# Stores of converted weight pieces queued two steps later, their raw weights fetched four products earlier, and the conversions of w_out spaced out

## The chip, the cores and the metric

The kernel runs as one program on one core of a Trainium2 chip. The metric is the device time of an execution in microseconds (us), as the median of three runs. TensorE (PE) multiplies; VectorE (DVE) and ScalarE (ACT) prepare operands and empty PSUM; SyncE (SP) issues every DMA.

## What is computed

A small attention in both directions between tokens and state, then two feed-forward layers over the 4352 rows that it gives. The change lies in the second of these layers and in the hand-over to it.

```python
def reference(x, state, w_in1, w_out1, s, b, w_in2, w_out2):
    x = attention(x, state)                     # 8*(512+32) = 4352 rows of 512
    h = np.maximum(x @ w_in1, 0.0)              # 512 -> 2048
    x = (s * (h * h) + b) @ w_out1              # 2048 -> 512
    h = np.maximum(x @ w_in2, 0.0)
    return (h * h) @ w_out2                     # what the changed code prepares and reads
```

## The kernel before, in words

Everything is fp32 to the caller. Each factor of a matmul is split into a rounded part "hi" and a remainder "lo" (hi is a copy on ACT, lo a subtraction on DVE), and three matmuls, hi by hi, hi by lo and lo by hi, stand for one.

The second layer works on 34 tiles of 128 rows in six parts of six tiles (the last has four). For each part the first matrix, w_in2, is gone through in eight **units** u of 256 columns (`units`, part by part; unit i of the whole list is written (i, m) with the step m inside it). A unit multiplies by Strassen's scheme in Winograd's form: seven **products** of half-size blocks, in the order `PRODUCTS`, one product being one step, m = 0 to 6. A product is six matmuls of 384 columns (L634). The products share two PSUM banks (psa and psb in turn), and some products add onto the bank of an earlier one, so product m = 3 can start only when DVE has taken product m = 1 out of its bank (the sum `r`, in the group DVE r L713), and m = 6 only when m = 4 has been taken out (`v`, DVE v L713). The first product of a unit goes into the bank of product m = 5 of the unit before, and the second (m = 1) into the bank of m = 6 of the unit before, which DVE empties with an add into `t`.

Between products PE does matmuls that are already prepared, its "flow": at the second of every two steps it takes ten or eleven matmuls with w_out2 (`mm2_second`, L679), which multiply what the unit before gave. So PE runs two products, some flow, two products, some flow. At the hand-over (unit 0) the flow is the last 24 matmuls of the first layer (L478), four of which are left for the first step of unit 1.

The weights of a unit are seven **pieces** (128x256, hi and lo beside each other), sums and differences of four blocks of w_in2. In the first part they have to be made. For units 0 and 1 that happens at steps of the first layer's last batch (`s8 + n`), for units u = 2 to 7 while unit u-1 is worked on:

- `sums_load(u)` (L527): two DMAs of 256 KB bring the raw blocks `ws` from HBM into tiles of a pool with four buffers. It was queued at (u-2, 6).
- `sums_add(u, n)` (L542, tiles `wt` and `ws`): three sums on DVE at (u-1, 0), one more at (u-1, 3).
- `sums_hi(u, m)` (L550, ACT) at (u-1, m), `sums_lo(u, m)` (L554, DVE) at (u-1, m+1). With the lo part, in the same function, went the DMA that stores the piece to HBM (L555, `w2s`), since parts 2 to 6 read the pieces from there (`w_load`, L563 and L566).

The pieces of even units lie in one set of places (behind the x operands in `xw`), those of odd units in another (`xw odd`).

The second matrix, w_out2, has been brought to fp32 in HBM earlier. It comes back in eight pieces of 512 KB, `load_w2` (L208, tile `o2f`), and is split by `cut`: `o2h` on ACT and `o2l` on DVE (L110, L111; 128x1024). Piece p holds the weights that unit p's results meet, and PE first reads it in unit p+1.

Nothing is reordered by a scheduler: every engine does its instructions in the order in which the code is run, and each of the engines' queues, SP's of DMAs too, waits at its head. The tables of steps (`at_step(step, fn, rank)` for the first layer, `then(i, m, fn)` and `between` for the second) thus set the order on DVE, ACT and SP at once.

Of the kernel before, what the change touches and what calls it, by code (L numbers as in the profile page):

```python
# [42 lines left out]
NF = DFF // P  # L43
NQ = 4
# [9 lines left out]
PRODUCTS = (1, 6, 2, 5, 7, 3, 4)  # L54
# [7 lines left out]
def attn_mlp2(ctx: ExitStack, tc: tile.TileContext, xT, xn, st, w_in1, w_out1, w_in2, w_out2, s_in, b_in, out):  # L62
# [43 lines left out]
    def raw4(name):  # L106
        return rawp.tile([P, 2, 512], F32, tag="raw", name=name)

    def split(hi, lo, src):
        nc.scalar.activation(out=hi, in_=src, func=ACTF.Copy)  # L110
        nc.vector.tensor_tensor(out=lo, in0=src, in1=hi.bitcast(F32), op=ALU.subtract)  # L111
# [53 lines left out]
    def w_tiles(key, q):  # L165
        if (key, q) not in W:
            W[key, q] = (w8([P, 4, 512], f"{key}h{q}"), w8([P, 4, 512], f"{key}l{q}"))
        return W[key, q]
# [37 lines left out]
    def load_w2(key, q, p):  # L206
        raw = raw4(f"{key}f{q}{p}")
        nc.sync.dma_start(out=raw, in_=w2_dr[key, q][:, 2 * p : 2 * p + 2, :])  # L208

        def cut():  # L210
            hi, lo = w_tiles(key, q)
            split(hi[:, 2 * p : 2 * p + 2, :], lo[:, 2 * p : 2 * p + 2, :], raw)

        return cut
# [301 lines left out]
    def w_at(e, m):  # L516

        return xw[m][:, 4 * TH :] if e == 0 else xw["odd", m // 4][:, m % 4 * 512 : m % 4 * 512 + 512]
# [3 lines left out]
    def sums_load(u):  # L522

        c0 = u % 2 * 2 * P
        sums[u] = [op.tile([P, 2, 2, P], F32, tag="o", name=f"ws{u}") for _ in range(2)]
        for d, t in enumerate(sums[u]):
            nc.sync.dma_start(  # L527
                out=t.rearrange("p i f c -> p i (f c)"),
                in_=w2_dr["i2", u // 2][:, 2 * d : 2 * d + 2, c0 : c0 + 2 * P],
            )  # L530

    def sums_add(u, n):

        (a11, a21), (a12, a22) = [[t[:, :, f, :] for f in range(2)] for t in sums[u][:2]]
        if n == 0:
            sums[u].append(an1.tile([P, 2, 2, P], F32, tag="an", name=f"wt{u}"))
        s1, s2 = (sums[u][2][:, i] for i in range(2))
        out, x, y, fn = (
            (s1, a21, a22, ALU.add), (s2, s1, a11, ALU.subtract),
            (a21, a11, a21, ALU.subtract), (a12, a12, s2, ALU.subtract),  # L540
        )[n]
        nc.vector.tensor_tensor(out=out, in0=x, in1=y, op=fn)  # L542
        sums[u, "src"] = {1: a11, 2: a12, 3: a12, 4: a22, 5: s1, 6: s2, 7: a21}

    def sums_view(u, m):
        return w_at(u % 2, m).rearrange("p (h i c) -> p h i c", h=2, i=2), sums[u, "src"][PRODUCTS[m]]

    def sums_hi(u, m):
        w, v = sums_view(u, m)
        nc.scalar.activation(out=w[:, 0], in_=v, func=ACTF.Copy)  # L550

    def sums_lo(u, m):
        w, v = sums_view(u, m)
        nc.vector.tensor_tensor(out=w[:, 1], in0=v, in1=w[:, 0].bitcast(F32), op=ALU.subtract)  # L554
        nc.sync.dma_start(out=w2s_dr[u][:, m, :], in_=w_at(u % 2, m).bitcast(F32))  # L555

    def w_load(i, m):
# [13 lines left out]
    def x_view(n, m):  # L571
        th = half(n)
        return xw[m][:, : 4 * th].rearrange("p (h i t) -> p h i t", h=2, i=2)
# [35 lines left out]
    def x_hi(n, m, i):  # L609
        nc.scalar.activation(out=x_view(n, m)[:, 0, i], in_=X["t", i][PRODUCTS[m]], func=ACTF.Copy)  # L610

    def x_lo(n, m, i):
        v = x_view(n, m)
        nc.vector.tensor_tensor(
            out=v[:, 1, i], in0=X["t", i][PRODUCTS[m]], in1=v[:, 0, i].bitcast(F32), op=ALU.subtract
        )
# [205 lines left out]
    def at_step(i, fn, rank=5):  # L822

        side.setdefault(i, []).append((rank, len(side.get(i, ())), fn))
# [5 lines left out]
    def step(j, f):  # L830
        return place[j, 0] + f
# [19 lines left out]
    rank = {att_sr: 0, att_tp: 0, att_sc: 0, att_put: 2, att_an: 3, att_turn: 3, att_exp: 5, att_norm: 5}  # L851
    for b in range(1, B):
# [6 lines left out]
        for q in range(NQ):  # L859

            n = base + 4 * q + 5 if b > 1 else (1, 12, 16, 20)[q]
# [28 lines left out]
    s8 = step(B, 0)  # L890
# [23 lines left out]
    for m in range(len(PRODUCTS)):  # L914
        n = s8 + (2, 2, 3, 5, 6, 9, 10)[m]
        for i in range(2):
            at_step(n, lambda m=m, i=i: x_hi(0, m, i), 8)
            at_step(n + 1, lambda m=m, i=i: x_lo(0, m, i), 6)
    for u, at0, steps in ((0, 4, (5, 5, 6, 6, 7, 9, 9)), (1, 11, (12, 12, 13, 13, 14, 14, 15))):
        at_step(s8 + 3, lambda u=u: sums_load(u), 9.5)  # L920
        for n in range(3):
            at_step(s8 + at0, lambda u=u, n=n: sums_add(u, n), 8)
        for m, n in enumerate(steps):
            at_step(s8 + n, lambda u=u, m=m: sums_hi(u, m), 9.5)
            at_step(s8 + n + 1, lambda u=u, m=m: sums_lo(u, m), 6)

        at_step(s8 + steps[2] + 1, lambda u=u: sums_add(u, 3), 7)
    between = {}
    w_pieces = {}
    for q in range(NQ):  # L930
        for h in range(2):

            load = lambda q=q, h=h: w_pieces.update({(q, h): load_w2("o2", q, h)})
            cut = lambda q=q, h=h: w_pieces.pop((q, h))()
            if q < 1:
                at_step(s8 + 11 + h, load, 9)
                at_step(s8 + 13 + h, cut, 9)
            else:
                between.setdefault((q - 1, 3 * h), []).append(load)
                between.setdefault((q - 1, 3 * h + 3), []).append(cut)  # L940

    def then(i, m, fn):
        between.setdefault((i + m // len(PRODUCTS), m % len(PRODUCTS)), []).append(fn)

    for u in range(2, NF // 2):
        then(u - 2, 6, lambda u=u: sums_load(u))
        for n in range(3):
            then(u - 1, 0, lambda u=u, n=n: sums_add(u, n))
        for m in range(len(PRODUCTS)):
            then(u - 1, m, lambda u=u, m=m: sums_hi(u, m))  # L950
            then(u - 1, m + 1, lambda u=u, m=m: sums_lo(u, m))
            if m == 2:
                then(u - 1, 3, lambda u=u: sums_add(u, 3))

# [10 lines left out]
    for f in range(1, NF):  # L965
        i = v_at[f] + (f >= VA)
# [128 lines left out]
```

## Time and profile before

| | us |
|---|---|
| median of three runs | 1420.15 (1417.08 to 1421.92) |
| the profiled execution | 1422.37 |
| its span in the trace | 1420.6 |

The profile is that of one execution. Times in it are counted from the start of the span. PE is the array's matmuls, PEld its weight loads, SPq the queue of DMAs on SP. "idle before <- X" names what ended an engine's wait. The granted clock (PEclk) is 1.00 when TensorE runs at 2.4 GHz and 0.50 at 1.2 GHz.

### The profile page before, as it was taken

Reading aid. Unit: us, or ns where it says so; the run is one execution under the profiler, and the core shown is the slowest. Engines: PE = TensorE matmul, PEld = TensorE weight load, DVE = VectorE, ACT = ScalarE, POOL = GpSimd, SP = SyncE. Lnnn points to the kernel's source line nnn. Section 1 sums busy time; section 2 is a strip of 40 time slices with the busy share of each in tenths; the row PEclk is TensorE's granted clock in tenths of the full one; section 3 lists DMA queues with packets and bytes.
Section 4 is the critical chain, followed back from the end, with each engine's and each line's share of the span. In section 5 each row is a group of like instructions: output and inputs, shape, how many; then the busy total and the mean of one; then the engine's idle time right before and its main releaser. Section 6 shows DMA issues by size and latency. Waiting matters only on the chain.

```text
span 1420.6 us, 20203 instructions
## 1 busy us (share of the span) xinstructions
PE 1380.5 (97%) x7770; PEld 1164.7 (82%) x7770; DVE 764.6 (54%) x1495; ACT 759.3 (53%) x1492; POOL 0.7 (0%) x7
## 2 busy tenths in 40 slices
PE   4999999999999999999988999999999999999998
PEld 2777777777777777889877889999999999989897
DVE  7888645555556766446655554353435344443533
ACT  4777656566666656557644543354345335433543
POOL 0000000000000000000000000000000000000000
PEclk7899999999999999999999999999999999999999
DMA  7365232423324142204563555445435544543652
GB/s 248 102 221 182 89 122 61 137 90 102 125 75 143 54 155 72 90 0 142 171 206 113 194 165 169 118 117 166 142 111 171 172 118 118 163 141 105 214 152 72
DMA packets 88863, 188.48 MB, mean 133 GB/s; under 512 B 8640, under 2 KB 26048, under 8 KB 86208
## 3 DMA queue, kind: packets, MB, share of 16 engines
q1 hardware_dynamic: 88768, 187.21, 41.6%
q8 instruction: 61, 1.00, 0.3%
q14 instruction: 34, 0.28, 0.1%
HBM read 144.18 MB, written 42.99 MB: 132 GB/s over the span
## 4 chain that ended last, share of the span: by engine, by line
PE 92%; DVE 3%; DMA 2%; ACT 1%; issue 1%; SPq 0%; DVEq 0%
PE acc L478 26%; PE o L679 25%; PE m L634 22%; PE h L448 14%; PE S L260 2%; DMA ws<-i 2%; PE sr L413 1%; PE sc L260 1%; PE S L288 1%; PE tp L393 0%; DMA o2f<-o 0%; DMA xT<-xT 0%; ACT sc L647 0%; SPq L527 0%; ACT o2h L110 0%
## 5 line engine op out<-in xcount | busy, mean ns | idle before, releaser
L478 PE MATMUL acc<-g,o1h 128*128 128x512 f32 (+1 forms) x1152 | 341.5, 379 | 0.0
L478 PEld LDWEIGHTS acc<-g,o1h 128*128 128x128 f32 x1152 | 211.7, 188 | 41.8 <-issue 2.2
L478 PE MATMUL acc<-g,o1l 128*128 128x512 f32 (+1 forms) x576 | 217.7, 378 | 0.4 <-DVE o1l L189 0.4
L448 PE MATMUL h<-aT,S 128*128 128x512 f32 x768 | 202.6, 399 | 5.8 <-DVE aT L387 3.2
L634 PE MATMUL m<-xw 128*128 128x384 f32 (+1 forms) x1008 | 185.9, 331 | 9.5 <-DVE r L713 8.0
L448 PEld LDWEIGHTS h<-aT,S 128*128 128x128 f32 x768 | 142.0, 189 | 61.0 <-issue 12.3
L634 PEld LDWEIGHTS m<-xw 128*128 128x128 f32 x1008 | 172.9, 190 | 18.1 <-DVE r L713 9.0
L647 ACT ACTIVATE sc<-sc 128x384 f32<-128x384 f32 (+1 forms) x144 | 72.7, 505 | 156.7 <-DVE sc L713 155.2
L461 DVE TENSOR_TENSOR g<-r,g 128x512 fp32r<-128x512 f32 (+1 forms) x144 | 94.8, 659 | 109.9 <-ACT g L457 109.9
L455 ACT ACTIVATE r<-h 128x512 f32<-128x512 f32 (+1 forms) x144 | 82.2, 571 | 124.5 <-PE h L448 124.4
L647 ACT ACTIVATE v<-m 128x384 f32<-128x384 f32 (+1 forms) x96 | 45.4, 473 | 152.1 <-PE m L634 151.6
L478 PEld LDWEIGHTS acc<-g,o1l 128*128 128x128 f32 x576 | 108.5, 188 | 21.3 <-DVE o1l L189 0.9
L679 PE MATMUL o<-o2h,xw('g', 0)_6303 128*128 128x512 f32 x364 | 122.3, 396 | 0.0
L679 PE MATMUL o<-o2h,xw('g', 1)_6304 128*128 128x512 f32 x364 | 121.2, 393 | 0.0
L679 PE MATMUL o<-o2h,xw('g', 2)_6305 128*128 128x512 f32 x360 | 120.1, 394 | 0.0
L713 DVE TENSOR_TENSOR v<-m,r 128x384 f32<-128x384 f32 (+1 forms) x48 | 25.7, 535 | 158.5 <-PE m L634 158.5
L634 PE MATMUL m<-xw,xw('odd', 0)_6178 128*128 128x384 f32 (+1 forms) x576 | 107.6, 328 | 3.1 <-DVE r L713 3.1
L634 PEld LDWEIGHTS m<-xw,xw('odd', 0)_6178 128*128 128x128 f32 x576 | 98.2, 188 | 8.0 <-DVE r L713 4.4
L457 ACT ACTIVATE g<-r 128x512 fp32r<-128x512 f32 (+1 forms) x144 | 87.7, 609 | 4.6
L456 ACT ACTIVATE r<-r 128x512 f32<-128x512 f32 (+1 forms) x144 | 87.7, 609 | 4.6
L111 DVE TENSOR_TENSOR S<-S,S 128x512 fp32r<-128x512 f32 x54 | 34.8, 687 | 91.4 <-ACT S L110 91.4
L634 PE MATMUL m<-xw,xw('odd', 1)_6179 128*128 128x384 f32 (+1 forms) x432 | 79.5, 327 | 0.6 <-DVE v L713 0.6
(146 smaller groups left out, 1900.0 us busy)
## 6 DMA issues: line engine op xcount, KB each, us to landing
xw<-w2s SPq DMA_DIRECT2D x140, 256.0 KB, 2.8
xw('odd', 0)_6178<-w2s SPq DMA_DIRECT2D x20, 1024.0 KB, 4.9
xw('odd', 1)_6179<-w2s SPq DMA_DIRECT2D x20, 768.0 KB, 4.3
i1r<-w_in SPq DMA_DIRECT2D x16, 512.0 KB, 4.7
xn<-xn SPq DMA_DIRECT2D x8, 1024.0 KB, 8.8
o1r<-w_out SPq DMA_DIRECT2D x16, 512.0 KB, 4.6
x<-ot SPq DMA_DIRECT2D x32, 256.0 KB, 3.1
i2r<-w_in SPq DMA_DIRECT2D x16, 512.0 KB, 5.3
```

What stands on the lines that cost most here:

```text
L111: nc.vector.tensor_tensor(out=lo, in0=src, in1=hi.bitcast(F32), op=ALU.subtract)
L260: nc.tensor.matmul(out=outs[r][k * NS : (k + 1) * NS], lhsT=state[rows, r, k, :], rhs=moving(rows, k), start=True, stop=True, skip_group_c ...
L448: nc.tensor.matmul(out=hp, lhsT=l_, rhs=r_, start=(i == 0), stop=(i == len(ops) - 1))
L455: nc.scalar.activation(out=r, in_=hp, func=ACTF.Relu)
L456: nc.scalar.activation(out=r, in_=r, func=ACTF.Square)
L457: nc.scalar.activation(out=g[:, 0], in_=r, func=ACTF.Copy)
L461: nc.vector.tensor_tensor(out=g[:, 1], in0=r, in1=g[:, 0].bitcast(F32), op=ALU.subtract)
L478: nc.tensor.matmul(out=o, lhsT=l_, rhs=r_, start=(opens and i == 0), stop=(closes and i == 2))
L634: nc.tensor.matmul(out=o, lhsT=w[:, a, k, :], rhs=x[:, b, k, :], start=(start and k + a + b == 0), stop=(k + a == 2), skip_group_check=True,)
L647: nc.scalar.activation(out=c, in_=src, func=func)
L679: nc.tensor.matmul(out=acc2[t], lhsT=l_, rhs=r_, start=(fa == 0 and e == 0), stop=(fa == NF - 1 and e == 2))
L713: add = lambda o, x, y: nc.vector.tensor_tensor(out=o, in0=x, in1=y, op=ALU.add)
```

## The change

The store of a piece becomes a function of its own, `sums_store`, which is put two steps behind the lo part. `sums_load(u)` moves from (u-2, 6) to (u-2, 2). The eight pieces of w_out2 are loaded and split at steps from a written table of (load, split) pairs, in which a number below zero is a step of the first layer and u = 7 stands for the steps of a unit; before, a loop put them at every third step. No instruction is added or removed and no size changes.

```diff
@@ -552,6 +552,8 @@
         w, v = sums_view(u, m)
         nc.vector.tensor_tensor(out=w[:, 1], in0=v, in1=w[:, 0].bitcast(F32), op=ALU.subtract)
+
+    def sums_store(u, m):
         nc.sync.dma_start(out=w2s_dr[u][:, m, :], in_=w_at(u % 2, m).bitcast(F32))
@@ -916,39 +918,46 @@
+    def behind(n, fn, rank):
+
+        if n < NF:
+            at_step(s8 + n, fn, rank)
+        else:
+            then(0, n - NF, fn)
+
     for u, at0, steps in ((0, 4, (5, 5, 6, 6, 7, 9, 9)), (1, 11, (12, 12, 13, 13, 14, 14, 15))):
         at_step(s8 + 3, lambda u=u: sums_load(u), 9.5)
         for m, n in enumerate(steps):
             at_step(s8 + n, lambda u=u, m=m: sums_hi(u, m), 9.5)
-            at_step(s8 + n + 1, lambda u=u, m=m: sums_lo(u, m), 6)
+            behind(n + 1, lambda u=u, m=m: sums_lo(u, m), 6)
+            behind(n + 3, lambda u=u, m=m: sums_store(u, m), 9.9)
-    for q in range(NQ):
-        for h in range(2):
-
-            load = lambda q=q, h=h: w_pieces.update({(q, h): load_w2("o2", q, h)})
-            cut = lambda q=q, h=h: w_pieces.pop((q, h))()
-            if q < 1:
-                at_step(s8 + 11 + h, load, 9)
-                at_step(s8 + 13 + h, cut, 9)
-            else:
-                between.setdefault((q - 1, 3 * h), []).append(load)
-                between.setdefault((q - 1, 3 * h + 3), []).append(cut)
+    u = len(PRODUCTS)
+    for p, (n, k) in enumerate((
+        (11 - NF, 14 - NF), (12 - NF, 1), (0, 5), (3, u + 1), (6, u + 4), (u + 2, 2 * u), (u + 5, 2 * u + 3),
+        (2 * u + 1, 2 * u + 6),
+    )):
+        q, h = p // 2, p % 2
+        behind(n + NF, lambda q=q, h=h: w_pieces.update({(q, h): load_w2("o2", q, h)}), 9)
+        behind(k + NF, lambda q=q, h=h: w_pieces.pop((q, h))(), 9)
     for u in range(2, NF // 2):
-        then(u - 2, 6, lambda u=u: sums_load(u))
+        then(u - 2, 2, lambda u=u: sums_load(u))
         for n in range(3):
             then(u - 1, 0, lambda u=u, n=n: sums_add(u, n))
         for m in range(len(PRODUCTS)):
             then(u - 1, m, lambda u=u, m=m: sums_hi(u, m))
             then(u - 1, m + 1, lambda u=u, m=m: sums_lo(u, m))
+            then(u - 1, m + 3, lambda u=u, m=m: sums_store(u, m))
```

What this does to SP's queue shows in unit 1. A row is a DMA, destination first; `w2s_2` are the stored pieces of unit 2 and `ws3` the raw blocks of unit 3. Before:

```order
L555 DMA w2s_2_119<-xw0_5737 128x512
L555 DMA w2s_2_119<-xw1_5738 128x512
L208 DMA o2f21_6507<-o2_2_115 128x1024
L555 DMA w2s_2_119<-xw2_5739 128x512
L555 DMA w2s_2_119<-xw3_5871 128x512
L555 DMA w2s_2_119<-xw4_5872 128x512
L555 DMA w2s_2_119<-xw5_6031 128x512
L527 DMA ws3_6578<-i2_1_110 128x2x256
L527 DMA ws3_6579<-i2_1_110 128x2x256
```

And in the changed kernel:

```order
L504 DMA x1_8_133<-ot_6430 128x256
L504 DMA x1_8_133<-ot_6436 128x256
L208 DMA o2f21_6488<-o2_2_115 128x1024
L527 DMA ws3_6492<-i2_1_110 128x2x256
L527 DMA ws3_6493<-i2_1_110 128x2x256
L557 DMA w2s_2_119<-xw0_5737 128x512
L557 DMA w2s_2_119<-xw1_5738 128x512
L208 DMA o2f30_6551<-o2_3_116 128x1024
```

The load of `ws3` stood behind six stores of unit 2's pieces and now stands ahead of all of them.

On DVE the second place is the start of unit 2, where product m = 1 is taken out (`r`, L713 before and L715 after), with the three sums for unit 3 ahead of it. Before:

```order
L661 TENSOR_TENSOR xw('g', 2)_6305<-sc,xw('g', 2)_6305 128x384
L644 SCALAR_TENSOR_TENSOR t_6544<-t_6544 128x384
L111 TENSOR_TENSOR o2l_6504<-o2f_6507,o2h_6503 128x1024
L554 TENSOR_TENSOR xw_6031<-ws_6413,xw_6031 128x256
L554 TENSOR_TENSOR xw_6032<-ws_6413,xw_6032 128x256
L542 TENSOR_TENSOR wt_6599<-ws_6578,ws_6579 128x256
L542 TENSOR_TENSOR wt_6599<-wt_6599,ws_6578 128x256
L542 TENSOR_TENSOR ws_6578<-ws_6578 128x2x128
L713 TENSOR_TENSOR r<-m_6604,v 128x384
```

And in the changed kernel:

```order
L663 TENSOR_TENSOR xw('g', 2)_6297<-sc,xw('g', 2)_6297 128x384
L646 SCALAR_TENSOR_TENSOR t_6546<-t_6546 128x384
L554 TENSOR_TENSOR xw_6026<-ws_6341,xw_6026 128x256
L111 TENSOR_TENSOR o2l_6532<-o2f_6488,o2h_6531 128x1024
L554 TENSOR_TENSOR xw_6027<-ws_6341,xw_6027 128x256
L542 TENSOR_TENSOR wt_6597<-ws_6492,ws_6493 128x256
L542 TENSOR_TENSOR wt_6597<-wt_6597,ws_6492 128x256
L542 TENSOR_TENSOR ws_6492<-ws_6492 128x2x128
L715 TENSOR_TENSOR r<-m_6602,v 128x384
```

The `o2l` moved behind one lo part. It now belongs to step (2, 0) instead of (1, 6), and so does its `o2h`, which stood on ACT among the hi parts of (1, 6) and stands there now behind the copy of unit 2's first product:

```order
L649 ACTIVATE v<-m_6580 128x384
L649 ACTIVATE t_6562<-t_6562 128x384 x2
L649 ACTIVATE xw('g', 0)_6295<-t_6562 128x384
L649 ACTIVATE xw('g', 0)_6295<-t_6546 128x384
L110 ACTIVATE o2h_6531<-o2f_6488 128x1024
L550 ACTIVATE xw('odd', 0)_6176<-ws_6492 128x256
```

Five instructions of ACT, which begin with that copy (`v`), now come between the first product of the unit and `o2l`. The third place is the end of unit 0 on DVE, where `t` empties the bank that unit 1's second product takes. Before:

```order
L713 TENSOR_TENSOR sc<-m_6340,r 128x384
L713 TENSOR_TENSOR t_6382<-v 128x384
L503 TENSOR_SCALAR ot<-acc_5762,s_sb 128x256
L713 TENSOR_TENSOR t_6406<-m_6364,r 128x384
L661 TENSOR_TENSOR xw('g', 0)_6303<-sc,xw('g', 0)_6303 128x384
L644 SCALAR_TENSOR_TENSOR t_6382<-t_6382 128x384
L111 TENSOR_TENSOR o2l_6359<-o2f_6362,o2h_6358 128x1024
```

And in the changed kernel:

```order
L715 TENSOR_TENSOR sc<-m_6344,r 128x384
L715 TENSOR_TENSOR t_6382<-v 128x384
L503 TENSOR_SCALAR ot<-acc_5762,s_sb 128x256
L111 TENSOR_TENSOR o2l_6401<-o2f_6310,o2h_6400 128x1024
L715 TENSOR_TENSOR t_6410<-m_6364,r 128x384
L663 TENSOR_TENSOR xw('g', 0)_6295<-sc,xw('g', 0)_6295 128x384
L646 SCALAR_TENSOR_TENSOR t_6382<-t_6382 128x384
```

An `o2l` stood behind the add that empties product m = 6 into `t`; one stands ahead of it now.

## Rows read from the trace of the kernel before

**Rows 1.** The page: busy time of PE, share of the span, instructions.

```profile
PE 1380.5 (97%) x7770; PEld 1164.7 (82%) x7770; DVE 764.6 (54%) x1495; ACT 759.3 (53%) x1492; POOL 0.7 (0%) x7
```

**Rows 2.** Busy time by stretch: each engine, PEclk, DMA share, GB/s.

```profile
800.00:820.00 20.00, 20.00 (x99) 17.81 (x99) 11.95 (x26) 11.78 (x26) 0.00 (x0) 1.00 0.52 175
```

**Rows 3.** Waits of 640 to 820: total us, times, longest.

```profile
PE m L634 <- DVE r L713: 11.1, 6, 3.8
PE m L634 <- DVE v L713: 2.1, 2, 1.5
DVE wt L542 <- DMA ws<-i: 26.3, 6, 6.5
```

**Rows 4.** PE in order of time: start, us; in brackets the idle time before.

```profile
691.37 1.33 PE L634 MATMUL m<-xw 128*128 128x384 f32 x6 [1.46 <-DVE v L713]
...
719.76 2.29 PE L634 MATMUL m<-xw 128*128 128x384 f32 x6 [2.93 <-DVE r L713]
...
758.27 1.97 PE L634 MATMUL m<-xw 128*128 128x384 f32 x5 [3.77 <-DVE r L713]
...
794.25 1.31 PE L634 MATMUL m<-xw 128*128 128x384 f32 x6 [1.30 <-DVE r L713]
```

**Rows 5.** The same view: the first products of units 0, 4 and 8.

```profile
681.13 2.25 PE L634 MATMUL m<-xw 128*128 128x384 f32 x12
748.87 2.27 PE L634 MATMUL m<-xw 128*128 128x384 f32 x12
820.23 2.27 PE L634 MATMUL m<-xw 128*128 128x384 f32 x12
```

**Rows 6.** The chain that ended last, in order of time: start, us.

```profile
671.21 1.44 PE acc L478 x12
...
815.75 2.10 PE m L634 x12
817.86 2.31 PE o L679 x10
```

**Rows 7.** SP's queue in order of time, in unit 4.

```profile
740.98 9.02 SPq L555 DMA_DIRECT2D w2s<-xw  x6
750.05 0.99 SPq L527 DMA_DIRECT2D ws<-i  x2
```

**Rows 8.** DVE in order of time, in unit 4.

```profile
756.53 0.42 DVE L542 TENSOR_TENSOR wt<-ws,ws 128x256 f32<-128x256 f32 x1 [6.55 <-DMA ws<-i]
...
757.67 0.55 DVE L713 TENSOR_TENSOR r<-m,v 128x384 f32<-128x384 f32 x1
```

**Rows 9.** ACT and DVE in order of time, in unit 0.

```profile
688.53 1.06 ACT L110 ACTIVATE o2h<-o2f 128x1024 fp32r<-128x1024 f32 x1 [0.86 <-DMA o2f<-o]
...
689.62 1.23 DVE L111 TENSOR_TENSOR o2l<-o2f,o2h 128x1024 fp32r<-128x1024 f32 x1 [5.58 <-ACT o2h L110]
```

**Rows 10.** Busy time by stretch, behind two of the gaps.

```profile
719.76:724.00 4.24, 4.24 (x14) 3.83 (x15) 1.55 (x4) 2.16 (x5) 0.00 (x0) 0.62 0.56 180
758.27:764.00 5.73, 5.73 (x15) 4.96 (x16) 3.25 (x8) 2.32 (x6) 0.00 (x0) 0.51 0.36 137
```

**Rows 11.** ACT and DVE in order of time, at starts of units and splits.

```profile
751.62 0.94 ACT L647 ACTIVATE xw('g', 1)_6304<-t 128x384 fp32r<-128x384 f32 x2
...
723.45 1.04 ACT L110 ACTIVATE o2h<-o2f 128x1024 fp32r<-128x1024 f32 x1
...
724.52 1.23 DVE L111 TENSOR_TENSOR o2l<-o2f,o2h 128x1024 fp32r<-128x1024 f32 x1 [3.21 <-ACT o2h L110]
725.67 0.42 DVE L554 TENSOR_TENSOR xw('odd', 0)_6178<-ws,xw('odd', 0)_6178 128x256 fp32r<-128x256 f32 x1
```

**Rows 12.** PE and DVE in order of time, at the end of unit 0.

```profile
686.84 2.25 PE L634 MATMUL m<-xw 128*128 128x384 f32 x12
...
691.70 0.55 DVE L713 TENSOR_TENSOR sc<-m,r 128x384 f32<-128x384 f32 x1
...
695.26 1.23 DVE L111 TENSOR_TENSOR o2l<-o2f,o2h 128x1024 fp32r<-128x1024 f32 x1 [0.28 <-ACT o2h L110]
```

More of the change, by code (lines that the diff above doesn't have):

```diff
@@ L918, in attn_mlp2, with then @@
             at_step(n + 1, lambda m=m, i=i: x_lo(0, m, i), 6)
+    between = {}
+    def then(i, m, fn):
+        between.setdefault((i + m // len(PRODUCTS), m % len(PRODUCTS)), []).append(fn)
+    def behind(n, fn, rank):
[3 more added lines that the diff above has]
+            then(0, n - NF, fn)
     for u, at0, steps in ((0, 4, (5, 5, 6, 6, 7, 9, 9)), (1, 11, (12, 12, 13, 13, 14, 14, 15))):
@@ L924, in attn_mlp2 @@
             at_step(s8 + n, lambda u=u, m=m: sums_hi(u, m), 9.5)
-            at_step(s8 + n + 1, lambda u=u, m=m: sums_lo(u, m), 6)
+            behind(n + 1, lambda u=u, m=m: sums_lo(u, m), 6)
+            behind(n + 3, lambda u=u, m=m: sums_store(u, m), 9.9)
         at_step(s8 + steps[2] + 1, lambda u=u: sums_add(u, 3), 7)
-    between = {}
     w_pieces = {}
-    for q in range(NQ):
-        for h in range(2):
-            load = lambda q=q, h=h: w_pieces.update({(q, h): load_w2("o2", q, h)})
-            cut = lambda q=q, h=h: w_pieces.pop((q, h))()
-            if q < 1:
-                at_step(s8 + 11 + h, load, 9)
-                at_step(s8 + 13 + h, cut, 9)
-            else:
-                between.setdefault((q - 1, 3 * h), []).append(load)
-                between.setdefault((q - 1, 3 * h + 3), []).append(cut)
-    def then(i, m, fn):
-        between.setdefault((i + m // len(PRODUCTS), m % len(PRODUCTS)), []).append(fn)
+    u = len(PRODUCTS)
[6 more added lines that the diff above has]
+        behind(k + NF, lambda q=q, h=h: w_pieces.pop((q, h))(), 9)
     for u in range(2, NF // 2):
-        then(u - 2, 6, lambda u=u: sums_load(u))
+        then(u - 2, 2, lambda u=u: sums_load(u))
         for n in range(3):
```

## The prediction

> **What bounds the kernel now.** I read the page first: PE is busy 97% of the span [rows 1], so only time in which PE stands or runs at its lower clock can be won. The table of busy time by stretches of 20 us then shows where that is. From 800 us on PE is busy all the time at the granted clock 1.00 [rows 2], and so it is in the stretches ahead of 680; the losses that this change can reach lie in units 0 to 7. The waits of that stretch say what they are: PE waits for DVE's `r` six times, 11.1 us in all, and for DVE's `v` twice, 2.1 us, together 13.2; the one row that stands beside them is DVE's own wait for the raw blocks `ws`, six times, 26.3 us [rows 3]. There is one such wait for each of the units u = 2 to 7.
>
> PE in order of time gives the sizes of the gaps, from 1.30 to 3.77 us in the four shown [rows 4], and DVE in order of time the cause: `wt` began 6.55 us late, for the DMA of `ws`, and `r`, which PE waits for, stands right behind the three sums [rows 8]. SP's queue shows why the DMA was late: six stores held its head for 9.02 us, each until DVE had made its lo part, and the loads behind them were issued at 750.05, 6.5 us before `wt` could start [rows 7, 8]. One gap has another cause: at 691.37 PE waits for `v` [rows 4], which stood on DVE behind an `o2l` that waited 5.58 us for its `o2h`, and that for the DMA of `o2f` [rows 9].
>
> **What all of this costs.** I take it from starts, since the idle times in the trace count from modelled ends of matmuls. Without a wait twelve matmuls of a product take 2.10 us, ten of the flow 2.31, and twelve of the first layer's last batch 1.44 [rows 6]: 0.175, 0.231 and 0.12 us each. Unit 0 is 42 product matmuls and 20 of the first layer, 7.35 + 2.40 = 9.75 us. A later unit is 42 and 36 of the flow, 7.35 + 8.32 = 15.67; unit 1 has four of the first layer more, 16.15. Units 0 to 7 should take 9.75 + 16.15 + 6 x 15.67 = 119.9 us. They took 820.23 - 681.13 = 139.1 [rows 5]. So **19.2 us** are to be had. The parts fit: 13.2 us of gaps, then 4.24 x 0.38 + 5.73 x 0.49 = 1.6 + 2.8 = 4.4 us that the lower clock cost behind the two long gaps [rows 10], and some 0.2 us at each of the eight restarts.
>
> **The loads, part one.** `sums_load` goes four products earlier, 4 x 15.67 / 7 = 9.0 us, and the stores that held the queue now ask for lo parts that DVE made two steps (4.5 us) before. The longest that DVE waited was 6.55 us [rows 8], so a lead of 9.0 covers each of the six, with 2.4 us to spare, if SP is not held by something else. What stands ahead of `ws` now are stores of lo parts already made and one load of `o2f`; for unit 3 also the four stores of the first layer's last rows, made in step (1, 0), and for unit 5 the eight DMAs that bring the next part's x. I cost these at nothing: `ws3` is not used before (2, 0) and the rows are out seven steps earlier. If this cover fails, the old gap at that unit stays. The wait for a free buffer is no new one: unit u takes the buffers of u-2, done with at (u-2, 0), two steps ahead of its load. The stores themselves are 42 + 14 DMAs of 256 KB as before, and PE waits for none of them. So the six gaps go, with the clock that fell behind two of them, and the smaller wait for `v` in unit 1, in which DVE was still catching up.
>
> **The splits of w_out2, part two.** Piece 1 is split later, at (0, 1) instead of a step of the first layer, and piece 2 at (0, 5) instead of (0, 3), with a longer lead behind its load. That removes the 5.58 us wait and the gap at 691.37. The splits at (0, 1), (1, 1), (1, 4), (2, 3) and (2, 6) I cost at nothing: there `o2l` stands behind the `r` or `v` of its step, and PE has a flow of 2.3 us and a product of 1.05 before it asks for the next one. Without that cover each would cost the 1.15 us from the start of `o2l` to that of DVE's next instruction [rows 11]. Two do not hide.
>
> At **(2, 0)** the `o2h` stands behind five ACT instructions that start with the end of unit 2's first product, and `o2l`, the last lo part, the three sums and `r` follow. Unit 4 of the old trace has the same ACT instructions at the same place: two products start at 748.87, and the last two copies before ACT is free at 751.62 take 0.94 [rows 5, 11]. Counted from the start of the first product, o2h starts at 2.75 + 0.85 = 3.6 (the next instruction starts about 0.1 before the end in the trace); o2l 1.07 behind it, 4.67; the next DVE instruction 1.15 on, 5.82 [rows 11]; the lo part 0.34 (0.42 less that overlap), 6.16; from `wt` to `r` 1.14, 7.30; and product m = 3 starts 0.60 behind `r`, at 7.90 [rows 4, 8]. PE could start it after 2.10 + 2.31 + 1.05 = 5.46. So a new gap of **2.4 us** comes to unit 2. Its bounds are nothing, should ACT run ahead, and 2.4 + 2.8 = 5.2, should the clock fall as it did behind the gap at 758.27.
>
> At **(0, 5)** an `o2l` now stands ahead of `t`, which must empty the bank before unit 1's second product. In the old trace o2l began 3.56 us after `sc`, behind the same ACT work [rows 12]. In the new one `sc` follows product m = 5, which ends at 686.84 + 2.25 = 689.09, say 689.17. Then o2l at 692.73, `t` at 693.88 and the product, by the same 0.60, at 694.48. PE could have started it at 686.84 + 2.10, plus seven matmuls of the first layer (0.84), two products (2.10), four more of the first layer (0.48) and five of the flow (1.16): 693.52. A new gap of **1.0 us**, bounded by nothing and by the 1.46 that an `o2l` cost at this place before [rows 4].
>
> **The sum.** 19.2 - 2.4 - 1.0 = 15.8 us less. The profiled execution took 1422.37, 2.2 us above the median; it would come to 1406.6, and the median to 1420.15 - 15.8 = **1404.4**. Three runs of before lie 4.8 us apart, and 0.3% (4.3 us) is about what a measurement of this kernel can tell from no change.
>
> **The rivals.**
> *The new gaps do not come* (ACT is ahead at both places): 1420.15 - 19.2 = 1401.0. For it speaks that ACT is busy only 53% of the time [rows 1]; against it that both chains start with PE itself. Chance 0.20.
> *The clock falls behind the gap at (2, 0).* Behind 2.93 and 3.77 us the granted clock was 0.62 and 0.51 over the next 4 to 6 us [rows 4, 10], the lower level of 1.2 GHz for most of them; behind 1.30 and 1.46 it stayed. A gap of 2.4 lies between. Cost 1.6 to 2.8: 1406.0 to 1407.2. Chance 0.22. The Trainium skill, in "TensorE: Matmul & The Clock Gate", section "Part 1: The HAM clock gate", says that the lower clock is the default and that only activity lifts it, so that a matmul stream starts slowly again after idle time; by that rule the new gap would cost this more. The two long gaps agree with it, and the short ones show that it does not follow every pause.
> *The loads are still late at some units*: `ws3` behind the four row stores, `ws5` behind the eight loads of x. If both old long gaps stay, 2.93 + 3.77 with 4.4 of clock, 11.1 us of the gain are missing: 1415.5. Against it stand the seven and six steps (some 13 us) between those DMAs and the use. Chance 0.08; that nearly all six waits stay and the change does no more than remove the 691.37 gap, 1418 to 1420, has 0.03.
> *Slower.* A store that is two steps later reads its piece two steps longer. `sums_hi(u+2, m)` writes the same place, 14 steps behind hi(u, m), and must wait for it: 11 steps, 24.6 us, lie between the two now, 13 before. If SP came to lag by more than that, ACT would wait in each of the units, and to lose the 15.8 us and 4.3 more over six units it must lag by 24.6 + 3.4 = 28 us. The longest that SP stood for stores was 9.02 us [rows 7], while they still waited for fresh lo parts. Chance 0.02: 1425.
>
> **How the numbers follow.** The forecast has 0.45; with the rivals above that is 1.00. The range takes in the first two rivals at both ends, with 2 us below and some 4 above for a set of three runs and for part of one late load: 1399 to 1411. That leaves out late loads, the slower case and a little of the spread. Faster by over 0.3%: 0.94; within: 0.04; slower: 0.02.
>
> **What would show it.** In the new trace the row of DVE waiting for `ws` is gone or below 2 us in all; SP's loads of `ws` are issued in the middle of the unit ahead; PE has two gaps between 681 and 805, one of about 1.0 us at the second product of unit 1 behind `t`, one of about 2.4 at the fourth of unit 2 behind `r`, each with an `o2l` just before on DVE; the granted clock is 1.00 in units 3 to 7; and unit 8 starts at 820.23 - 15.8 = 804.4. Wrong would be: gaps at the fourth product of units 3 to 6 behind `wt`, or ACT waiting for a `w2s` store ahead of L550.

## The result and the profile after

The changed kernel takes **1405.8 us** (median of four runs, 1405.25 to 1406.81) against 1420.27 of the kernel before on the same chip: a ratio of 0.9902, with a 95% interval of 0.9883 to 0.992. The forecast was 1404.4. The profiled execution took 1405.25 us with a span of 1403.5.

The waits of the same stretch as in [rows 3], in the changed kernel (total us, times, longest). There is no row of DVE waiting for `ws` any more, and PE's waits, 13.2 us before, are two:

```profile
PE m L636 <- DVE r L715: 2.3, 1, 2.3
...
PE m L636 <- DVE t L715: 0.8, 1, 0.8
```

PE in order of time, as in [rows 4, 5] (start, us; in brackets the idle time before): the first products of unit 0 and of unit 8, and between them the only two gaps, at the second product of unit 1 and at the fourth of unit 2, whose third stands ahead of it and whose next pair of products behind it:

```profile
679.67 2.25 PE L636 MATMUL m<-xw 128*128 128x384 f32 x12
...
692.98 2.35 PE L636 MATMUL m<-xw,xw('odd', 0)_6176 128*128 128x384 f32 x12 [0.83 <-DVE t L715]
...
710.95 1.23 PE L636 MATMUL m<-xw 128*128 128x384 f32 x6
714.43 1.33 PE L636 MATMUL m<-xw 128*128 128x384 f32 x6 [2.25 <-DVE r L715]
...
717.91 2.27 PE L636 MATMUL m<-xw 128*128 128x384 f32 x12
...
803.12 2.27 PE L636 MATMUL m<-xw 128*128 128x384 f32 x12
```

Units 0 to 7 take 803.12 - 679.67 = 123.45 us instead of 139.1. By starts the gaps are a little larger than the idle times: the fourth product of unit 2, at 714.43, could have started 1.05 behind 710.95, at 712.00, and started 2.43 later. Busy time by stretch (each engine, PEclk, DMA share, GB/s) shows that the clock stayed up behind both:

```profile
680.00:700.00 20.00, 19.17 (x113) 18.15 (x112) 13.81 (x28) 12.67 (x26) 0.00 (x0) 1.00 0.67 209
700.00:720.00 20.00, 17.75 (x88) 15.69 (x88) 12.02 (x24) 11.68 (x25) 0.00 (x0) 1.00 0.61 212
720.00:740.00 20.00, 20.00 (x101) 17.84 (x100) 15.48 (x35) 11.05 (x25) 0.00 (x0) 1.00 0.70 227
```

SP's queue in order of time says where the wait went that answered to [rows 7]. `ws3` and `ws4` (L527) go out at 696.30 and 713.21:

```profile
696.30 1.48 SPq L527 DMA_DIRECT2D ws<-i  x2
...
713.21 0.98 SPq L527 DMA_DIRECT2D ws<-i  x2
...
730.60 11.44 SPq L557 DMA_DIRECT2D w2s<-xw  x7
742.09 1.01 SPq L527 DMA_DIRECT2D ws<-i  x2
```

The queue still stands for stores, here 11.44 us for seven of them, longer than the 9.02 before; but the `ws` behind them, issued at 742.09, are not read before 757.48. DVE and ACT in order of time show the two new gaps as forecast, each an `o2l` that waits for its `o2h` ahead of what PE needs:

```profile
691.23 1.23 DVE L111 TENSOR_TENSOR o2l<-o2f,o2h 128x1024 fp32r<-128x1024 f32 x1 [2.15 <-ACT o2h L110]
692.38 0.55 DVE L715 TENSOR_TENSOR t<-m,r 128x384 f32<-128x384 f32 x1
...
710.14 1.04 ACT L110 ACTIVATE o2h<-o2f 128x1024 fp32r<-128x1024 f32 x1
...
711.21 1.23 DVE L111 TENSOR_TENSOR o2l<-o2f,o2h 128x1024 fp32r<-128x1024 f32 x1 [4.42 <-ACT o2h L110]
...
712.69 0.42 DVE L542 TENSOR_TENSOR wt<-ws,ws 128x256 f32<-128x256 f32 x1
...
713.82 0.55 DVE L715 TENSOR_TENSOR r<-m,v 128x384 f32<-128x384 f32 x1
```

`ws3`, issued at 696.30, is read at 712.69, 16.4 us later, without a wait; in unit 4 of the kernel before, DVE stood until 6.5 us behind the issue [rows 7, 8].

### The profile page after: what moved, and what is told of

Same layout as the page of the kernel before. It is cut to its first block, busy times and chain, and to the rows that moved or that the text cites. A ratio compares the mean times of both kernels' runs of the same rounds, so it can differ in the third digit from the quotient of the medians.

```text
span 1403.5 us, 20210 instructions
## 1 busy us (share of the span) xinstructions
PE 1371.6 (98%) x7770; PEld 1159.5 (83%) x7770; DVE 765.1 (55%) x1495; ACT 759.1 (54%) x1492; POOL 0.7 (0%) x7
## 4 chain that ended last, share of the span: by engine, by line
PE 95%; DVE 3%; ACT 1%; DMA 0%; issue 0%; SPq 0%
PE o L681 27%; PE acc L478 26%; PE m L636 24%; PE h L448 14%; PE S L260 2%; PE sr L413 1%; PE sc L260 1%; PE tp L393 0%; PE S L288 0%; DMA xT<-xT 0%; DVE m L362 0%; DVE t L376 0%; DVE t L363 0%; DVE V L141 0%; DVE V L146 0%
## 5 line engine op out<-in xcount | busy, mean ns | idle before, releaser
L448 PE MATMUL h<-aT,S 128*128 128x512 f32 x768 | 201.9, 397 | 6.2 <-DVE aT L387 3.5
L448 PEld LDWEIGHTS h<-aT,S 128*128 128x128 f32 x768 | 141.4, 189 | 60.9 <-issue 9.2
L681 PE MATMUL o<-o2h,xw('g', 0)_6295 128*128 128x512 f32 x364 | 121.2, 392 | 0.0
L681 PE MATMUL o<-o2h,xw('g', 1)_6296 128*128 128x512 f32 x364 | 121.1, 392 | 0.0
L681 PE MATMUL o<-o2h,xw('g', 2)_6297 128*128 128x512 f32 x360 | 119.7, 392 | 0.0
L715 DVE TENSOR_TENSOR v<-m,r 128x384 f32<-128x384 f32 (+1 forms) x48 | 25.7, 536 | 164.4 <-PE m L636 164.4
L636 PE MATMUL m<-xw,xw('odd', 0)_6176 128*128 128x384 f32 (+1 forms) x576 | 107.4, 328 | 0.8 <-DVE t L715 0.8
L636 PEld LDWEIGHTS m<-xw,xw('odd', 0)_6176 128*128 128x128 f32 x576 | 98.3, 188 | 5.0 <-DVE t L715 1.2
L636 PE MATMUL m<-xw,xw('odd', 1)_6177 128*128 128x384 f32 (+1 forms) x432 | 79.3, 327 | 0.0
```

The source lines that it names most:

```text
L448: nc.tensor.matmul(out=hp, lhsT=l_, rhs=r_, start=(i == 0), stop=(i == len(ops) - 1))
L636: nc.tensor.matmul(out=o, lhsT=w[:, a, k, :], rhs=x[:, b, k, :], start=(start and k + a + b == 0), stop=(k + a == 2), skip_group_check=True,)
L681: nc.tensor.matmul(out=acc2[t], lhsT=l_, rhs=r_, start=(fa == 0 and e == 0), stop=(fa == NF - 1 and e == 2))
L715: add = lambda o, x, y: nc.vector.tensor_tensor(out=o, in0=x, in1=y, op=ALU.add)
```

## The experiments

The theory to test, the queue theory: PE's gaps come from raw weights that stand in SP's queue behind stores which wait for lo parts, and the gaps that stay come from two splits of w_out2. Its rivals: that the splits carry the gain, that only one of the two moves counts or both are needed, and that a store that comes late makes ACT wait.

| kernel | units 0 to 7, us | PE's gaps, us idle | median, us | ratio to before |
|---|---|---|---|---|
| before | 139.10 | eight, 13.2 in all | 1420.27 to 1421.22 | |
| changed | 123.45 | 0.83, 2.25 | 1405.8 | 0.9902 (0.9883 to 0.992) |
| e1 splits only | 136.26 | seven, 11.5 in all | 1419.57 | 0.9986 (0.9975 to 0.9997) |
| e2 loads only | 123.11 | 1.70, 0.70 | 1405.52 | 0.9887 (0.9872 to 0.9901) |
| e3 stores only | 122.61 | 0.48, 0.87, 0.61 | 1405.78 | 0.989 (0.9875 to 0.9904) |
| e4 loads and stores | 122.10 | 0.48, 1.23 | 1404.91 | 0.9881 (0.9864 to 0.9897) |
| e5 two splits moved | 119.83 | none | 1403.52 | 0.9877 (0.9862 to 0.9891) |
| e6 changed again | 123.43 | 0.83, 2.25 | 1406.1 | 0.9897 (0.9882 to 0.9911) |
| e7 two splits at (2, 0) | 125.96 | 3.39 | 1408.0 | 0.9906 (0.9891 to 0.9921) |
| e8 stores five steps late | 119.84 | none | 1402.49 | 0.9872 (0.9855 to 0.9888) |

The second column is the distance of the first products of units 0 and 8, as read above.

**e1: only the splits.** Against the changed kernel:

```diff
-            behind(n + 3, lambda u=u, m=m: sums_store(u, m), 9.9)
+            behind(n + 1, lambda u=u, m=m: sums_store(u, m), 9.9)
-        then(u - 2, 2, lambda u=u: sums_load(u))
+        then(u - 2, 6, lambda u=u: sums_load(u))
-            then(u - 1, m + 3, lambda u=u, m=m: sums_store(u, m))
+            then(u - 1, m + 1, lambda u=u, m=m: sums_store(u, m))
```

> Only the new table of splits of w_out2; stores go with their lo parts and raw weights are loaded at (u-2, 6) as before. Queue theory (PE's gaps come from the raw weights standing in SP's queue behind stores that wait for lo parts): the six waits of DVE for ws stay at 24 to 28 us in all, the gap of 1.46 us before unit 1's first product goes, one of about 1.0 at unit 1's second product comes; the o2l at (2, 0) costs nothing, since DVE waits for ws there anyway. About 0.5 us less than before: 1419 to 1421. Rival (the splits themselves hold DVE up and carry a good part of the gain): 1408 to 1415.

Its waits of 640 to 830 (total us, times, longest), PE in order of time at units 2 and 4, and the stretch behind the gap in unit 2 by engine (as above, the granted clock is third from the end):

```profile
DVE wt L542 <- DMA ws<-i: 22.7, 5, 6.2
...
717.75 1.31 PE L636 MATMUL m<-xw 128*128 128x384 f32 x6 [2.25 <-DVE r L715]
...
722.78 2.24 PE L636 MATMUL m<-xw 128*128 128x384 f32 x12
...
755.95 1.62 PE L636 MATMUL m<-xw 128*128 128x384 f32 x6 [3.42 <-DVE r L715]
...
717.75:722.78 5.03, 5.03 (x17) 4.18 (x18) 2.79 (x6) 3.26 (x7) 0.00 (x0) 0.66 0.63 206
```

The waits for `ws` stay, five of them and 22.7 us where 24 to 28 were expected, and the gain is small: 2.0 us by the ratio (its interval allows 0.4 to 3.6) and 2.84 in the eight units of the trace, where 0.5 were expected. Of the 2.84, 1.54 are won in units 0 and 1, where the gap behind `v` in unit 1 (0.62 before) went along with the 1.46. At unit 2 the `o2l` of (2, 0) makes DVE later than the raw weights did, so the wait for `ws3` is hidden, and the gap of 2.93 became the 2.25 of the changed kernel: 0.67 us. The remaining 0.65 come from unit 4 on. The splits alone do not carry the gain.

The clock is another matter. Behind this gap of 2.25 us it fell: 0.66 over the next 5.03 us. From the fourth product to the next pair PE took 5.03 us, and in the changed kernel, behind the same gap at the same product, 717.91 - 714.43 = 3.48. The fall cost 1.55 us here and nothing there.

**e2: only the loads.** The two stores as in e1, and the old places of the splits, written as a table:

```diff
-        (11 - NF, 14 - NF), (12 - NF, 1), (0, 5), (3, u + 1), (6, u + 4), (u + 2, 2 * u), (u + 5, 2 * u + 3),
-        (2 * u + 1, 2 * u + 6),
+        (11 - NF, 13 - NF), (12 - NF, 14 - NF), (0, 3), (3, 6), (u, u + 3), (u + 3, u + 6), (2 * u, 2 * u + 3),
+        (2 * u + 3, 2 * u + 6),
```

> Only the loads of raw weights moved to (u-2, 2); stores with their lo parts and splits of w_out2 as before. Queue theory: a load now stands behind two stores of its unit instead of six, whose lo parts are made about nine us before the sums, so all six waits go with the lower clock behind them; the gap of 1.46 us at 691 stays. 19.2 - 1.5 = 17.7 us less than before: 1401.5 to 1404.5, a little below the changed kernel. Rival (the load must also be clear of stores that still wait): half of the DVE wait stays, 1408 to 1414.

No row of waiting for `ws` is left. PE in order of time:

```profile
690.10 1.33 PE L636 MATMUL m<-xw 128*128 128x384 f32 x6 [1.70 <-DVE v L715]
...
704.98 1.33 PE L636 MATMUL m<-xw,xw('odd', 1)_6179 128*128 128x384 f32 x6 [0.70 <-DVE v L715]
```

The loads alone take all six waits away. They win 16.0 us in the eight units and 15.7 by the medians, where 17.7 were expected, and the median is 1 us above the range. One reason is a second gap that I had thought would go with the waits, at the last product of unit 1, behind `v`.

**e3: only the stores.** The loads at (u-2, 6) as in e1, the old splits as in e2.

> Only the stores moved two steps behind their lo parts; raw weights loaded at (u-2, 6) and splits of w_out2 as before. Queue theory: the load stands behind the fourth store instead of the sixth, two steps or 4.5 us earlier in lo parts, so waits of 2.5 to 6.6 us shrink to at most 2.1 and PE has gaps of at most 1 us at one or two units; the granted clock stays 1.00. 15 to 18 us less than before: 1402 to 1405. Rival (the load's own place decides): the six waits stay, 1415 to 1420.

Its waits for `ws` and PE's gaps, in order of time:

```profile
DVE wt L542 <- DMA ws<-i: 2.0, 2, 1.6
...
690.53 1.31 PE L636 MATMUL m<-xw 128*128 128x384 f32 x6 [0.48 <-DVE v L715]
699.81 0.44 PE L636 MATMUL m<-xw,xw('odd', 0)_6176 128*128 128x384 f32 x1 [0.87 <-DVE r L715]
...
706.14 1.31 PE L636 MATMUL m<-xw,xw('odd', 1)_6177 128*128 128x384 f32 x6 [0.61 <-DVE v L715]
```

The stores alone take 24 of the 26.3 us of waiting away, though no load stands at another step. In the eight units 16.5 us are won and by the medians 15.4, both within the 15 to 18 expected. The median itself is 0.8 us above the range of 1402 to 1405, which was reckoned from a median of 1420.15 for the kernel before; beside this run that kernel took 1421.22. The gap behind `v` in unit 1 stands here too, 0.61 us.

**e4: loads and stores.** The changed kernel with the old splits of e2.

> Loads and stores moved, splits of w_out2 as before. Queue theory: no wait for ws, no gap at unit 1's second product and none at unit 2's fourth, since both belong to the new splits; the gap before unit 1's first product (o2l at (0, 3) waiting for its load) shrinks to 0 to 1.3 us, because the load stands behind four stores instead of seven. 17.5 to 19 us less than before: 1401 to 1403, two to three below the changed kernel. Rival (the spread splits are needed to keep DVE free): gaps at other units, 1406 or more.

No wait for `ws` is left, and neither new gap comes: both belong to the new splits. But 1.23 us stay at the end of unit 1, and the median is 1.9 us above the 1401 to 1403 expected. PE's gap there, and ACT and DVE in order of time:

```profile
705.42 1.31 PE L636 MATMUL m<-xw,xw('odd', 1)_6177 128*128 128x384 f32 x6 [1.23 <-DVE v L715]
...
701.78 1.06 ACT L110 ACTIVATE o2h<-o2f 128x1024 fp32r<-128x1024 f32 x1 [0.50 <-DMA o2f<-o]
...
702.88 1.23 DVE L111 TENSOR_TENSOR o2l<-o2f,o2h 128x1024 fp32r<-128x1024 f32 x1 [3.85 <-ACT o2h L110]
...
704.81 0.55 DVE L715 TENSOR_TENSOR v<-m,r 128x384 f32<-128x384 f32 x1
```

DVE did not come late from anything: it stood 3.85 us idle ahead of the `o2l` of (1, 3), with `v` behind it. The `o2h` that it waited for stands on ACT behind copies of a product, and waited 0.50 us more for its load; e3 has no such wait, and 0.61 us of gap instead of 1.23. The new table has that split at (1, 4), behind `v`. So the old splits cost two gaps (0.48 and 1.23 here), and the new ones take both away for two others.

**e5: two splits moved.** Against the changed kernel:

```diff
-        (11 - NF, 14 - NF), (12 - NF, 1), (0, 5), (3, u + 1), (6, u + 4), (u + 2, 2 * u), (u + 5, 2 * u + 3),
+        (11 - NF, 14 - NF), (12 - NF, 1), (0, 6), (3, u + 1), (6, u + 4), (u + 2, u + 6), (u + 5, 2 * u + 3),
```

> The changed kernel with two of the eight splits of w_out2 at other steps: piece 2 at (0, 6) instead of (0, 5), behind the add into t on DVE; piece 5 at (1, 6) instead of (2, 0), ahead of the copy of unit 2's first product on ACT. If the two new gaps (0.83 and 2.25 us of idle time) come from these o2l, both go and none takes their place: units 0 to 7 take 119.9 to 120.5 us instead of 123.45, and the median is 1401.5 to 1403.5. Rival (DVE has no room left there, so the wait only moves): a gap of 0.5 us or more behind r or v in units 1 or 2, and 122 us or more.

The first products of units 0 and 8, and the stretch between by engine, as above:

```profile
680.24 2.25 PE L636 MATMUL m<-xw 128*128 128x384 f32 x12
...
800.07 2.27 PE L636 MATMUL m<-xw 128*128 128x384 f32 x12
...
680.00:820.00 140.00, 140.00 (x717) 127.39 (x716) 92.91 (x198) 81.32 (x180) 0.00 (x0) 1.00 0.60 197
```

PE is busy for all of the 140 us. The eight units take 119.83 us; the count of matmuls had given 119.9. The four runs (1402.21 to 1403.93) lie below all four of the changed kernel beside them (e6, 1405.54 to 1406.68).

**e6: the changed kernel again.**

> The changed kernel once more, beside the others on the same chip: 1404 to 1407, units 0 to 7 in 123.2 to 123.7 us with the gaps at the second product of unit 1 and the fourth of unit 2 again. A rival that takes these gaps for chance of one execution expects them at other places or of other sizes.

The two gaps come back at the same places and with the same sizes to 0.01 us.

**e7: two splits at (2, 0).** Against e5:

```diff
-        ... (6, u + 4), (u + 2, u + 6), (u + 5, 2 * u + 3),
+        ... (6, 2 * u), (u + 2, 2 * u), (u + 5, 2 * u + 3),
```

> As the kernel with two splits moved, but pieces 4 and 5 are both split at (2, 0). By the chain that priced the gap there (first product, copies, o2h, o2l, lo part, sums, r) a second o2l adds its 1.15 us: product m = 3 of unit 2 starts 3.6 us late, 3.4 of it shown as idle time. The old kernel's gaps of 2.93 and 3.77 were followed by a granted clock of 0.5, so here it should fall, for 1.6 to 2.8 us more: units 0 to 7 in 125 to 126.5 us. Rival (the clock stays up in this stretch, as behind 2.25): 123.3 to 123.8. Rival (o2l is not on the chain): 122.5 or less.

The gap in PE's order of time, and the stretch behind it by engine:

```profile
714.68 2.29 PE L636 MATMUL m<-xw 128*128 128x384 f32 x6 [3.39 <-DVE r L715]
...
714.68:720.60 5.92, 5.92 (x16) 5.11 (x17) 2.71 (x6) 3.27 (x7) 0.00 (x0) 0.54 0.54 178
```

One more `o2l` makes the gap 1.14 us longer, as expected, and now the granted clock is 0.54 over the next 5.92 us, the lower level of 1.2 GHz for nearly all of them: 5.92 x 0.46 = 2.7 us. Units 0 to 7 take 6.1 us more than in e5, 3.6 for the gap by starts and 2.5 for the clock. One of the four runs (1405.41) is 2.5 us shorter than the other three (1407.95 to 1408.37), with a mean granted clock of 0.991 against 0.988; that would fit a run in which the clock did not fall, but no trace of it was kept.

**e8: stores five steps late.** Against e5:

```diff
-            behind(n + 3, lambda u=u, m=m: sums_store(u, m), 9.9)
+            behind(n + 6, lambda u=u, m=m: sums_store(u, m), 9.9)
-            then(u - 1, m + 3, lambda u=u, m=m: sums_store(u, m))
+            then(u - 1, m + 6, lambda u=u, m=m: sums_store(u, m))
```

> As the kernel with two splits moved, but each store stands five steps behind its lo part instead of two, which leaves 8 steps (18 us) before the hi copy that writes the place again. Queue theory: no difference, units 0 to 7 in 119.9 to 120.5 us. Rival (a late store makes ACT wait for the place of the piece, which was the way to a slower kernel): ACT waits for a w2s store ahead of L550, 121 us or more.

119.84 us against 119.83, and ACT has no wait for a store. Against e5 the medians do not tell (1402.04 to 1403.44 and 1402.21 to 1403.93).

## Why the prediction was right, and where not

**What could be won.** Right. 119.9 us was counted for units 0 to 7 without a wait; e5 and e8 measure 119.83 and 119.84.

**The loads.** Right that all six waits go, with the clock that fell behind two of them. Shown by e1, where load and store stay and so do five of the waits (the sixth is hidden), and by e2 to e4. What the prediction did not see is that either move alone is nearly enough: the longer lead (e2, no wait left) or the queue free of fresh stores (e3, 2.0 us left). It priced their sum, which is the same; whoever had added up two gains would have counted the 15 us twice.

**The smaller wait for v in unit 1.** Right that it goes, wrong why. The prediction put it to DVE "still catching up" after the wait for `ws`. In e2 and e4 nothing waits for `ws`, and it is there, 0.70 and 1.23 us; in e1 the waits for `ws` are back and it is gone. It belonged to the split at (1, 3), and went because that split moved.

**The splits.** The gap at 691 went, as forecast. Two things can shrink it: in e3 and e4, with the old splits, the load of the piece stands behind fewer stores, and 0.48 us are left of 1.46. The two splits that do not hide were found with their sizes: 1.0 forecast and 0.96 measured at unit 1's second product (by starts: 692.98 against 689.33 + 1.05 + 0.48 + 1.16 = 692.02), 2.4 and 2.43 at unit 2's fourth. The second was right link by link: counted from 706.53, the start of the unit's first pair of products, `o2h`, `o2l`, `r` and the product were forecast 3.6, 4.67, 7.30 and 7.90 us on and began 3.61, 4.68, 7.29 and 7.90 on. e5, which moves these two splits and nothing else, loses both gaps; e7 adds the 1.15 us for a second `o2l`.

**The clock.** The forecast left it up behind a gap of 2.4 us, and in both profiles of the changed kernel (this one and e6) it stayed at 1.00. That was a choice between rows, and it was luck in part: in e1 the clock fell behind the same 2.25 us at the same product, for 1.55 us, which is about the lower price (1.6) of the rival that had 0.22. So the length of the gap did not settle it; what did is not shown. Behind 2.93 and 3.77 us (before), 3.42 (e1) and 3.39 (e7) it fell each time, to 0.62, 0.51, 0.66 and 0.54 over the next 4 to 6 us. The Trainium skill's rule in "TensorE: Matmul & The Clock Gate", section "Part 1: The HAM clock gate", that the slow clock is the default and activity lifts it, agrees with e1 and e7 (0.66 and 0.54 behind the gap); the same 2.25 us in the changed kernel and e6 show again that it does not follow every pause.

**The other rivals.** New gaps do not come: they came. Loads still late: `ws3` had 16 us of lead. Slower by late stores: not by five steps (e8); further was not tried.

**The sum.** In the eight units 139.10 - 123.45 = 15.65 us were won where 15.8 were forecast. The profiled execution fell by 17.1 us, the median by 14.5. For the profiles the traces account: 15.65 in the units, and 1.46 because unit 0 starts at 679.67 instead of 681.13. That second part has nothing to do with the change. It arises in the first 60 us, where all ten kernels are the same: six matmuls of L448 start at 61.25 in the kernel before and at 59.80 in the changed one (59.75 to 61.45 in all ten), and in each profile unit 0 follows 619.9 us behind them. In these 60 us the granted clock is not steady, and from 40 to 50 us it was 0.64 in the kernel before and 0.96 in the changed one; the row tends to start later where it was lower.

For the medians this scatter of 1.7 us is not enough. The runs of the changed kernel spread over 1.6 us, but the thirteen of the kernel before beside e1 over 6.9 (1417.19 to 1424.08). The forecast took 4.4 us for the two falls of the clock from one execution, 2.2 us above the median, as if every run had them. A run of the kernel before in which one of them did not come would be shorter by 1.6 or 2.8, and e1 shows that the same gap can come with the fall or without it. For those runs that is an inference: only one execution of the kernel before was profiled.

## What to carry to other kernels

A store that is queued the moment its data are ordered held everything behind it in that queue here until they were made. Either queue it a step or two later or bring the loads forward, and expect the two remedies to win the same time once (16.5 and 16.0 us in the eight units alone, 17.0 together). When work is spread over "free" steps, look at what stands behind it on its engine: in this kernel a split behind the instruction that PE waits for cost nothing (e5), one ahead of it made DVE late by its own length and by the wait for its `o2h` (a gap of 2.25 us in the changed kernel), and a second one by 1.14 us more (e7). Count what the stretch would take without a wait from a few rows of undisturbed matmuls first: it says how much there is to find, and whether all of it was found (119.9 counted, 119.83 in e5).

## What was not expected of the hardware

The price of an idle gap of PE jumps, and its length does not say on which side it lands: 2.25 us of idle time at one and the same product cost themselves alone in the changed kernel and in e6, and 1.55 us more for the clock in e1. All four longer gaps, of 2.93 to 3.77 us, cost more than themselves. And SP's queue may stand 11.44 us for stores without a loss, if the loads behind it are far enough ahead of their use (12 to 16 us in the changed kernel).
